# MLP products and transposes as pairs of 128x64 column tiles, and constants from a scan on VectorE

## The chip, the cores and the metric

One core of a Trainium2 chip. The metric is device time of one execution in microseconds (us), a little under 2 us more than the span from first to last instruction that the profile shows. The medians are of all executions; six of these were classed slow (one each in e1, e3, e5 and e10, two in e11), and the ratios leave them out. PE is TensorE's matmuls, PEld its weight loads, DVE is VectorE, ACT is ScalarE, POOL is GpSimd, SP is SyncE.

## The reference

Retention (attention with a decay instead of a softmax) over 8 batches, 8 heads, 576 positions and head size 64, followed by an MLP with the exact GELU over 4,608 tokens, width 512, inner width 2,048.

```python
scores = scale * np.matmul(q, k.transpose(0, 1, 3, 2))
ret = scores * Dmat[None, :, :, :]           # gamma ** (i - j) for i >= j, else 0
attn_out = np.matmul(ret, v)
x = attn_out.transpose(0, 2, 1, 3).reshape(B * S, H * D)
h = x @ w_in
g = 0.5 * h * (1.0 + erf(h / sqrt(2)))
out = g @ w_out
```

## The kernel before

The sequence is cut into 40 chunks of 128 positions (the last of each batch has 64). For each chunk q, k and v are loaded by POOL, q and k are turned (on PE for the first 9 chunks, by DMA transpose after that), and PE computes scores, inner products, running states and a cross term. Their sum, scaled, is xT, the input of the MLP. The MLP products use one level of Strassen-like sums: `hT` is the first product, `fast` the second, `lean` the first one of the last two token blocks. A list schedule written in Python mixes attention groups into the MLP by a modelled clock, so the kernel's instruction order is fixed when it is built.

Three shapes of TensorE array appear. The MLP and the transposes use the whole array:

```python
        tiled(0)                                   # only the schedule's model of a mode change
        hT, tag = bank([128, TOK_BLK], FP32, "hT")
        ...
        for cc in range(N_DM):
            nc.tensor.matmul(hT[:, :hi - lo], lhsT=w[:, cc, o:o + 128], rhs=xT[:, cc, ...],
                             start=(cc == 0), stop=(cc == N_DM - 1))
```

Inner products and states use two column tiles of 128x64, scores and cross four or two tiles of 64x64:

```python
                nc.tensor.matmul(s["o_ps"][64 * e:64 * e + 64, hp, :cs], lhsT=s["vh"][:, 2 * hp + e, :],
                                 rhs=s["ret"][e][:, hp, :cs], ...)          # inner, 128x64
                    nc.tensor.matmul(sc[e][lo:lo + 64, hp, :cs], lhsT=qkT[sl, 1, hp, lo:lo + 64],
                                     rhs=qkT[sl, 0, hp, :cs], ...)          # scores, 64x64
```

The constants (identity, mask, positions, decay factors) are made at the start by POOL, PE and VectorE together; POOL makes the identity between its first two loads:

```python
    nc.gpsimd.dma_start(qk0[:, 1], k[0, :, 0:C, :].rearrange("h s d -> s h d"))
    make_identity(nc, ident)
    nc.gpsimd.dma_start(v0, v[0, :, 0:C, :].rearrange("h s d -> s h d"))
    ...
    nc.gpsimd.iota(pos[:, 0, :], ...)
    nc.gpsimd.affine_select(out=msk[:, 0, :], ...)
```

## Time and profile before

| | before |
|---|---|
| time, median of 3 (range) | 293.27 us (292.81 to 295.05) |
| span of the profiled run | 291.2 us |
| PE busy | 279.8 us, 96% |
| changes of array mode, counted from the matmuls' shapes | 80 |
| first MLP matmul | at 18.0 us |
| instruction fetches of 16 KB | 26 |

The page of the kernel before. Part 1 gives busy time and instruction counts, part 2 tenths of busy time in 40 slices of the span, part 3 a DMA queue with its packets, MB and share of the span.

```profile
span 291.2 us, 8057 instructions
...
PE 279.8 (96%) x3374; PEld 211.3 (73%) x3390; DVE 216.7 (74%) x492; ACT 139.3 (48%) x291; POOL 112.6 (39%) x143
...
PE   6879999999999999999999999999999999999995
...
PEclk9999999999999999999999999999999999999999
...
q8 instruction: 26, 0.43, 0.6%
```

PE is busy everywhere but in the first slices, at full clock.

The timeline of the kernel before around one attention group: start, duration, engine, line, operation, shapes.

```profile
83.83 0.39 PE L389 MATMUL u_ps<-vh,qk_ld 128*64 128x64 bf16 x14
...
84.05 0.62 PE L366 MATMUL o_ps<-ret,vh 128*64 128x128 bf16 x16
...
84.60 0.64 PE L330 MATMUL sc<-qkT 64*64 64x128 bf16 x32
...
85.07 0.39 PE L422 MATMUL o_ps<-qkT,u_sb 64*64 64x128 bf16 x8
...
85.39 0.83 PE L574 MATMUL fast<-w_sum,g 128*128 128x256 bf16 x6
```

The array goes from 128x128 (before the first line) to 128x64, to 64x64 and back: three changes. In single matmuls, the start-to-start time is 109 ns for 256 columns and 202 ns when the next matmul has another shape: 93 ns a change. (The count of 80 takes the one short transpose, 64x128, for a full tile. The trace shows such gaps, 95 ns on entering and 91 ns on leaving it, so 81 is as good a count.)

POOL at the start of the kernel before:

```profile
1.31 1.03 POOL L113 DMA_DIRECT2D qk_ld<-in_k_dram  x1 [0.80 <-POOLq L1008]
2.33 0.23 POOL masks.py:197 MEMSET ident<- 128x128 bf16 x1
2.63 0.29 POOL masks.py:199 TENSOR_SCALAR_AFFINE_SELECT ident<-ident 128x128 bf16<-128x128 bf16 x1
2.87 0.92 POOL L116 DMA_DIRECT2D v_ld<-in_v_dram  x1
...
4.14 0.91 POOL L224 DMA_DIRECT2D qk_ld<-in_q_dram  x1
```

The identity and later the positions and mask hold the loads back by 0.9 us.

### The profile page before, as it was taken

The page shows a single profiled execution, that of the slowest core. Times are in us where ns is not written, and L with a number is a line of the kernel's source. Part 1 is how long each engine was busy: PE and PEld are TensorE (multiplying, and loading weights), DVE is VectorE, ACT ScalarE, POOL GpSimd, SP SyncE. Part 2 cuts the span into 40 slices and gives each one's busy share as a digit, 9 for nine tenths or more (in the row PEclk, how much of TensorE's full clock was granted, in tenths as well). Part 3 has the DMA queues.
Part 4 walks back from the last instruction along what each step waited for, and adds up shares of the span by engine and source line. Part 5 has one row for each costly group of instructions (what it writes and reads, how often), then busy time and mean ns, then how long its engine had stood idle before and what let it go on. Part 6 is the DMA issues. An engine that isn't in the chain of part 4 may idle for free.

```text
span 291.2 us, 8057 instructions
## 1 busy us (share of the span) xinstructions
PE 279.8 (96%) x3374; PEld 211.3 (73%) x3390; DVE 216.7 (74%) x492; ACT 139.3 (48%) x291; POOL 112.6 (39%) x143
## 2 busy tenths in 40 slices
PE   6879999999999999999999999999999999999995
PEld 2555687888988788557865586559854888888884
DVE  5865896928849997997299917979596778995552
ACT  3755584622426721554236523552246438787221
POOL 8978876967366327526743525000000000000000
PEclk9999999999999999999999999999999999999999
DMA  9999999999999999999999999960210000300133
GB/s 87 136 172 185 178 176 186 145 160 138 181 197 188 170 145 149 184 184 159 124 186 175 154 144 157 164 78 2 74 74 0 1 2 0 146 0 3 50 132 108
DMA packets 153605, 35.65 MB, mean 122 GB/s; under 512 B 142305, under 2 KB 149473, under 8 KB 153569
## 3 DMA queue, kind: packets, MB, share of 16 engines
q0 software_dynamic: 117872, 18.23, 91.9%
q1 hardware_dynamic: 35696, 16.91, 33.2%
q8 instruction: 26, 0.43, 0.6%
q14 instruction: 11, 0.08, 0.1%
HBM read 36.70 MB, written 9.44 MB: 158 GB/s over the span
## 4 chain that ended last, share of the span: by engine, by line
PE 81%; DVE 11%; POOL 4%; DMA 2%; issue 1%; POOLq 0%; DVEq 0%
PE fast L574 34%; PE hT L469 29%; PE lean L707 8%; PE sc L330 3%; PE o_ps L366 2%; DVE ret L341 2%; DMA w_in<-in_moe_w_in_dram 2%; PE u_ps L389 2%; PE o_ps L422 2%; POOL qk_ld L224 2%; DVE s L506 2%; DVE s L505 1%; DVE s L508 1%; DVE s L507 1%; DVE xT L434 1%
## 5 line engine op out<-in xcount | busy, mean ns | idle before, releaser
L469 PE MATMUL hT<-xT,w_in 128*128 128x512 bf16 (+5 forms) x646 | 101.1, 309 | 2.5 <-DMA w_in<-in_moe_w_in_dram 1.1
L473 ACT ACTIVATE g<-hT 128x512 bf16<-128x512 f32 (+6 forms) x165 | 73.8, 460 | 51.7 <-PE hT L469 49.9
L469 PEld LDWEIGHTS <-w_in 128*128 128x128 bf16 x660 | 56.0, 98 | 40.8 <-DMA w_in<-in_moe_w_in_dram 2.1
L574 PEld LDWEIGHTS <-s 128*128 128x128 bf16 x576 | 56.0, 98 | 7.4 <-DVE s L506 0.7
L574 PE MATMUL fast<-w_sum,s 128*128 128x256 bf16 x432 | 49.4, 273 | 0.3 <-DVE s L506 0.2
L224 POOL DMA_DIRECT2D qk_ld<-in_q_dram x39 | 33.4, 857 | 33.6 <-DMA qkT<-qk_ld 18.9
L574 PEld LDWEIGHTS <-g 128*128 128x128 bf16 x432 | 41.6, 98 | 5.7
L341 DVE TENSOR_TENSOR ret<-sc,msk 128x512 bf16<-128x512 f32 x64 | 41.0, 683 | 0.9 <-PE sc L330 0.8
L224 POOL DMA_DIRECT2D v_ld<-in_v_dram x39 | 33.2, 853 | 18.4 <-DVE ret L341 4.6
L224 POOL DMA_DIRECT2D qk_ld<-in_k_dram x39 | 33.4, 856 | 10.0 <-DMA v_ld<-in_v_dram 9.0
L574 PE MATMUL fast<-w_out,g 128*128 128x256 bf16 x288 | 33.6, 273 | 0.1
L598 DVE TENSOR_TENSOR o_sb<-fast,u 128x512 f32<-128x512 f32 (+1 forms) x20 | 12.7, 634 | 26.8 <-PE fast L574 16.9
L594 ACT COPY u<-fast 128x512 f32<-128x512 f32 (+1 forms) x20 | 10.9, 544 | 39.6 <-PE fast L574 39.6
L434 DVE TENSOR_TENSOR xT<-o_ps,dq 128x512 bf16<-128x512 f32 (+1 forms) x42 | 24.0, 605 | 0.0
L351 DVE TENSOR_TENSOR vh<-v_ld,dv 128x512 bf16<-128x512 bf16 x32 | 21.3, 682 | 2.7 <-DMA v_ld<-in_v_dram 2.7
L505 DVE TENSOR_TENSOR s<-g 128x512 bf16<-128x512 bf16 x36 | 15.1, 420 | 5.5 <-ACT g L473 5.1
L574 PE MATMUL fast<-w_out,s 128*128 128x256 bf16 x144 | 17.3, 272 | 0.0
L574 PE MATMUL fast<-w_sum,g 128*128 128x256 bf16 x144 | 17.3, 273 | 0.0
L404 ACT CAST u_sb<-run_sum 128x256 bf16<-128x256 f32 x24 | 9.7, 405 | 15.2 <-DVE run_sum L401 11.7
L506 DVE TENSOR_TENSOR s<-s,g 128x512 bf16<-128x512 bf16 x36 | 15.3, 425 | 1.2
L507 DVE TENSOR_TENSOR s<-g 128x512 bf16<-128x512 bf16 x36 | 15.1, 419 | 0.0
L508 DVE TENSOR_TENSOR s<-g,s 128x512 bf16<-128x512 bf16 x36 | 15.1, 418 | 0.0
(85 smaller groups left out, 295.7 us busy)
## 6 DMA issues: line engine op xcount, KB each, us to landing
out_dram<-o_sb SPq DMA_DIRECT2D x16, 512.0 KB, 7.1
qk_ld<-in_k_dram POOLq DMA_DIRECT2D x32, 128.0 KB, 8.9
v_ld<-in_v_dram POOLq DMA_DIRECT2D x32, 128.0 KB, 8.6
qk_ld<-in_q_dram POOLq DMA_DIRECT2D x31, 128.0 KB, 8.9
w_in<-in_moe_w_in_dram POOLq DMA_DIRECT2D x8, 256.0 KB, 7.5
w_out<-in_moe_w_out_dram POOLq DMA_DIRECT2D x8, 256.0 KB, 7.7
out_dram<-o_sb SPq DMA_DIRECT2D x8, 128.0 KB, 1.7
qk_ld<-in_q_dram POOLq DMA_DIRECT2D x8, 64.0 KB, 8.5
```

The source lines that it names most:

```text
L224: nc.gpsimd.dma_start(dst[:cs], src[b, :, c0:c0 + cs, :].rearrange("h s d -> s h d"))
L341: nc.vector.tensor_tensor(r[:cs, :, :cs], sc[e][:cs, :, :cs], msk[:cs, :, :cs].to_broadcast([cs, HP, cs]), op=ALU.mult)
L351: nc.vector.tensor_tensor(vh[:cs], loaded[i][1][:cs], dv[:cs, :, ci:ci + 1].to_broadcast([cs, H, D]), op=ALU.mult)
L434: nc.vector.tensor_tensor(xT[:, :, at:at + hi - lo], s["o_ps"][:, :, lo:hi], dq[:, :, c0 + lo:c0 + hi], op=ALU.mult)
L469: nc.tensor.matmul(hT[:, :hi - lo], lhsT=w[:, cc, o:o + 128], rhs=xT[:, cc, tok0 % RING + lo:tok0 % RING + hi], start=(cc == 0), stop=(cc ...
L473: nc.scalar.activation(g_of(t, m, lo, hi), hT[:, :hi - lo], AF.Gelu)
L505: nc.vector.tensor_tensor(u[:, 0], a[2, 1], a[2, 2], op=ALU.add)
L506: nc.vector.tensor_tensor(u[:, 1], u[:, 0], a[1, 1], op=ALU.subtract)
L507: nc.vector.tensor_tensor(u[:, 2], a[1, 1], a[2, 1], op=ALU.subtract)
L508: nc.vector.tensor_tensor(u[:, 3], a[1, 2], u[:, 1], op=ALU.subtract)
L574: nc.tensor.matmul(acc_[:, p, :], lhsT=left(t, lhs, j, p), rhs=right(rhs, j), start=(fresh and j == 0 and (p == 0 or apart)), stop=(j == N ...
L707: nc.tensor.matmul(acc_[:, p, :], lhsT=left_, rhs=right_, start=(k in (1, 2, 7) and cc == 0 and p == 0), stop=(cc == 1), skip_group_check= ...
```

## The change

Its intent: if MLP and transposes run as pairs of 128x64 tiles, the change between 128x128 and 128x64 falls away and only scores and cross still need one. And if VectorE makes the constants with a scan (a running count along the row), POOL can issue loads at once.

```diff
     def mlp1_step(t, m, lo, hi):
-        tiled(0)
+        tiled(1)
...
-            nc.tensor.matmul(hT[:, :hi - lo], lhsT=w[:, cc, o:o + 128], rhs=xT[...],
-                             start=(cc == 0), stop=(cc == N_DM - 1))
+            for sl in HALVES:                      # slice(0, 64), slice(64, 128)
+                nc.tensor.matmul(hT[sl, :hi - lo], lhsT=w[:, cc, o + sl.start:o + sl.stop], rhs=xT[...],
+                                 start=(cc == 0), stop=(cc == N_DM - 1), skip_group_check=True)
... (the same in the second product, the lean blocks and the transposes)
-    make_identity(nc, ident)
-    nc.gpsimd.dma_start(v0, ...)
+    nc.gpsimd.dma_start(v0, ...)
+    nc.vector.tensor_tensor_scan(row, ones.to_broadcast([128, S]), ones.to_broadcast([128, S]), -1.0,
+                                 op0=ALU.mult, op1=ALU.add)
... (identity, mask and positions from row and its 32x32 transpose; iota, affine_select and
     the product on PE go; six warm-up matmuls at once; three memsets moved behind the first mask)
```

More of the change, by code (lines that the diff above doesn't have):

```diff
@@ L7 @@
 from concourse import bass_utils, mybir
-from concourse.masks import make_identity
 from concourse._compat import with_exitstack
@@ L65 @@
     TR_LEAD = 5
+    POOL_0 = 2.0
+    LAND_0 = (2.9, 4.0, 5.0)
+    CLOCK_0 = 3.2
     PLAN = [(1, 16), (1, 5), (1, 110), (0, 103), (1, 60), (1, 26), (1, 55), (0, 6), (2, 1), (1, 91), (0, 61), (1, 28), (2, 40), (2, 20), (2, 1), (1, 0), (2, 71), (2, 10), (2, 70), (2, 91), (2, 119), (2, 73), (2, 129), (2, 147), (2, 76), (2, 178), (2, 111), (1, 155), (0, 0), (0, 0)]
@@ L113 @@
     nc.gpsimd.dma_start(qk0[:, 1], k[0, :, 0:C, :].rearrange("h s d -> s h d"))
+    nc.gpsimd.dma_start(v0, v[0, :, 0:C, :].rearrange("h s d -> s h d"))
+    ones = const_pool.tile([128, 1], FP32, name="ones")
+    nc.vector.memset(ones, 1.0)
+    row = o_pool.tile([128, S], FP32, tag="o_sb0", name="row", bufs=2)
+    nc.vector.tensor_tensor_scan(row, ones.to_broadcast([128, S]), ones.to_broadcast([128, S]), -1.0,
+                                 op0=ALU.mult, op1=ALU.add)
+    colp = const_pool.tile([128, 1], FP32, name="colp")
+    for n in range(4):
+        nc.vector.memset(colp[32 * n:32 * n + 32], 32.0 * n)
+    turned = const_pool.tile([128, 32], FP32, name="turned")
+    nc.vector.transpose(turned, row[:, :32])
+    nc.vector.tensor_tensor(colp, colp, turned[:, 0:1], op=ALU.add)
     ident = const_pool.tile([128, 128], BF16, name="ident")
-    make_identity(nc, ident)
-    nc.gpsimd.dma_start(v0, v[0, :, 0:C, :].rearrange("h s d -> s h d"))
+    nc.vector.tensor_scalar(ident, row[:, :128], colp, None, op0=ALU.is_equal)
     lg_row = const_pool.tile([128, H, 1], FP32, name="lg_row")
@@ L120 @@
         nc.vector.memset(lg_row[:, h], log_gamma[h])
+    lg_col = const_pool.tile([128, HP], FP32, name="lg_col")
+    for e in range(2):
+        sl = slice(64 * e, 64 * e + 64)
+        nc.vector.tensor_copy(lg_col[sl], lg_row[sl, e::2, 0])
     ln_scale = const_pool.tile([128, 1], FP32, name="ln_scale")
     nc.vector.memset(ln_scale, math.log(scale))
-    msk = const_pool.tile([128, 1, 128], FP32, name="msk")
-    nc.vector.memset(msk, 1.0)
-    pos = const_pool.tile([128, 1, NCH], FP32, name="pos")
-    nc.gpsimd.iota(pos[:, 0, :], pattern=[[C, NCH]], base=0, channel_multiplier=1,
-                   allow_small_or_imprecise_dtypes=True)
-    nc.gpsimd.affine_select(
-        out=msk[:, 0, :], in_=msk[:, 0, :], compare_op=ALU.is_ge, fill=0.0, base=0,
-        pattern=[[1, 128]], channel_multiplier=-1,
-    )
-    lg_col = const_pool.tile([128, HP], FP32, name="lg_col")
-    for h in range(H):
-        e, hp = h % 2, h // 2
-        nc.vector.memset(lg_col[64 * e:64 * e + 64, hp:hp + 1], log_gamma[h])
-    base = const_pool.tile([128, NCH, 1], FP32, name="base")
-    for c in range(NCH):
-        nc.vector.memset(base[:, c], float(C * c))
-    ones = const_pool.tile([128, 128], BF16, name="ones")
-    nc.vector.memset(ones, 1.0)
-    ret_short = [const_pool.tile([128, HP, 128], BF16, name=f"ret_short{e}") for e in range(2)]
-    vh_short = const_pool.tile([128, H, D], BF16, name="vh_short")
-    for t in ret_short + [vh_short]:
-        nc.vector.memset(t, 0.0)
-    diag = const_pool.tile([128, 128], BF16, name="diag")
-    nc.vector.tensor_tensor(diag, ident, pos[:, 0, 0:1].to_broadcast([128, 128]), op=ALU.mult)
+    nc.vector.tensor_copy(qk0[:, 0], first)
+    pos = const_pool.tile([128, 1, NCH], FP32, name="pos")
+    nc.vector.tensor_tensor(pos[:, 0], row[:, 0::C], colp.to_broadcast([128, NCH]), op=ALU.add)
+    arg = const_pool.tile([128, H, NCH], FP32, name="arg")
+    nc.vector.tensor_tensor(arg, lg_row.to_broadcast([128, H, NCH]), pos.to_broadcast([128, H, NCH]), op=ALU.mult)
+    msk = const_pool.tile([128, 1, 128], FP32, name="msk")
+    nc.vector.tensor_scalar(msk[:, 0], row[:, :128], colp, None, op0=ALU.is_ge)
     warm_ps = ps.tile([128, 512], FP32, tag="f", name="warm")
-    row_ps = ps.tile([128, 1, 128], FP32, tag="g", name="row_ps")
     def warm_up(n):
@@ L155, in warm_up @@
             nc.tensor.matmul(warm_ps, lhsT=zeros[:, :128], rhs=zeros, start=True, stop=True)
-    warm_up(4)
-    nc.tensor.matmul(row_ps[:, 0], lhsT=ones, rhs=diag, start=True, stop=True)
-    row = o_pool.tile([128, NCH, 128], FP32, tag="o_sb0", name="row", bufs=2)
-    nc.vector.tensor_tensor(row, row_ps.to_broadcast([128, NCH, 128]), base.to_broadcast([128, NCH, 128]), op=ALU.add)
-    arg = const_pool.tile([128, H, NCH], FP32, name="arg")
-    nc.vector.tensor_tensor(arg, lg_row.to_broadcast([128, H, NCH]), pos.to_broadcast([128, H, NCH]), op=ALU.mult)
+    warm_up(6)
     dv = const_pool.tile([128, H, NCH], FP32, name="dv")
@@ L167 @@
     for hp in range(HP):
-        nc.scalar.activation(dq[:, hp], row.rearrange("p c s -> p (c s)")[:, :S], AF.Exp, scale=lg_col[:, hp:hp + 1])
+        nc.scalar.activation(dq[:, hp], row, AF.Exp, scale=lg_col[:, hp:hp + 1])
     warm_act = const_pool.tile([128, 1], FP32, name="warm_act")
     nc.scalar.activation(warm_act, ln_scale, AF.Gelu)
+    ret_short = [const_pool.tile([128, HP, 128], BF16, name=f"ret_short{e}") for e in range(2)]
+    vh_short = const_pool.tile([128, H, D], BF16, name="vh_short")
     loaded = {}
@@ L178 @@
     dma_at = [0.0]
-    pool_at = [3.3]
+    pool_at = [POOL_0]
     def serve(queues, t, until, landed):
@@ L217, in load_chunk @@
             loaded[i] = (qk0, v0)
-            nc.vector.tensor_copy(qk0[:, 0], first)
-            land_q[i], land_k[i], land_v[i] = on_dve(4.25, 512, 1.5), 5.3, 6.2
+            land_q[i], land_k[i], land_v[i] = on_dve(LAND_0[0], 512, 1.5), LAND_0[1], LAND_0[2]
             return
@@ L276, in bank @@
         return ps.tile(shape, dtype, tag=tag, name=name), tag
-    mode = [0]
+    mode = [1]
+    HALVES = (slice(0, 64), slice(64, 128))
     def tiled(n):
@@ L299, in turn @@
             return
-        tiled(0)
+        tiled(1 if cs == C else 2)
         for j in parts:
@@ L304, in turn @@
             for hp in range(HP):
-                nc.tensor.transpose(ps_[:, hp, :cs], qk[:cs, j, 2 * hp:2 * hp + 2, :], ident[:cs, :cs])
+                for e, sl in enumerate(HALVES):
+                    nc.tensor.transpose(ps_[sl, hp, :cs], qk[:cs, j, 2 * hp + e, :], ident[:cs, :cs])
             clock[0] += 0.23 * cs / C
@@ L464, in mlp1_step @@
         wait(x_ready(tok0 + lo, tok0 + hi))
-        tiled(0)
+        tiled(1)
         hT, tag = bank([128, TOK_BLK], FP32, "hT")
@@ L468, in mlp1_step @@
         for cc in range(N_DM):
-            nc.tensor.matmul(hT[:, :hi - lo], lhsT=w[:, cc, o:o + 128], rhs=xT[:, cc, tok0 % RING + lo:tok0 % RING + hi],
-                             start=(cc == 0), stop=(cc == N_DM - 1))
+            for sl in HALVES:
+                nc.tensor.matmul(hT[sl, :hi - lo], lhsT=w[:, cc, o + sl.start:o + sl.stop],
+                                 rhs=xT[:, cc, tok0 % RING + lo:tok0 % RING + hi],
+                                 start=(cc == 0), stop=(cc == N_DM - 1), skip_group_check=True)
         clock[0] += N_DM * ((hi - lo) / 2400 + 0.0028)
@@ L565, in fast_step @@
         wait(fast_ready(t, n))
-        tiled(0)
+        tiled(1)
         if k in (1, 2, 7) and (p == 0 or apart):
@@ L573, in fast_step @@
         for j in range(N_DF // 2):
-            nc.tensor.matmul(acc_[:, p, :], lhsT=left(t, lhs, j, p), rhs=right(rhs, j),
-                             start=(fresh and j == 0 and (p == 0 or apart)), stop=(j == N_DF // 2 - 1),
-                             skip_group_check=True)
+            for sl in HALVES:
+                nc.tensor.matmul(acc_[sl, p, :], lhsT=left(t, lhs, j, p)[:, sl], rhs=right(rhs, j),
+                                 start=(fresh and j == 0 and (p == 0 or apart)), stop=(j == N_DF // 2 - 1),
+                                 skip_group_check=True)
         clock[0] += 0.1092 * (N_DF // 2)
@@ L691, in lean_step @@
         end = f["end"]
-        tiled(0)
+        tiled(1)
         if k in (1, 2, 7):
@@ L706, in lean_step @@
                 right_ = x_part(t, int(rhs[1]), int(rhs[2]))[:, cc] if rhs[0] == "B" else x_sums[t][int(rhs[1]) - 1][:, cc]
-                nc.tensor.matmul(acc_[:, p, :], lhsT=left_, rhs=right_, start=(k in (1, 2, 7) and cc == 0 and p == 0),
-                                 stop=(cc == 1), skip_group_check=True)
+                for sl in HALVES:
+                    nc.tensor.matmul(acc_[sl, p, :], lhsT=left_[:, sl], rhs=right_,
+                                     start=(k in (1, 2, 7) and cc == 0 and p == 0), stop=(cc == 1), skip_group_check=True)
         clock[0] += 4 * 0.1092
@@ L909, in attend @@
                 masked(new[0])
+            if new[:1] == [0]:
+                for t in ret_short + [vh_short]:
+                    nc.vector.memset(t, 0.0)
+                    on_dve(clock[0], 256, 1.2)
             for j in pend:
@@ L972 @@
     weights_due = [(land_out[7] + 2.0, 0, 4), (land_out[7] + 6.0, 4, 8)]
-    warm_up(2)
-    clock[0] = 4.2
+    clock[0] = CLOCK_0
     while True:
```

## The prediction

> **What bounds the kernel now.** TensorE, except at the start. The page gives PE 96% busy of a 291.2 us span at a granted clock of 1.00, and from 50 us on nearly every slice is 90% or more. The chain of waits that ended last is 81% PE. Reading start-to-start times of single matmuls out of the trace: a full 128x128 matmul costs 216 ns at 512 columns, 109 ns at 256, 56 ns at 128. Summing streaming time over all 3374 recorded matmuls gives about 261 us. About 18 us remains as stalls (some of it records that are missing), 12 us of it before 50 us. There the timeline shows PE waiting for loads; the first w_in tile landed at 17.9 us. The remaining 7.4 us are changes of array mode.
>
> **What a change of mode costs.** [...] 109 ns becomes 202 ns at a change, 216 becomes 309, 82.5 becomes 176. That is 93 ns each. There are 80: about 25 triples (128x128 to 128x64, to 64x64, and back).
>
> **What the change does to PE.** With MLP and most transposes in 128x64, the triple becomes a pair: 27 entries to 64x64 and 27 exits are left, so 24 to 26 changes fall away (one short transpose keeps 64x64). 26 x 93 ns = 2.4 us, all on PE, hence nearly all on the critical path.
>
> **What it adds.** MLP products (about 1,900 matmuls) become pairs, so as many more matmuls and weight loads. [...] I expect no time from it: the inner products in this trace already run as 128x64 pairs, second tile 3 to 4 ns after the first, one pair per 56 ns at 128 columns, as one full matmul takes; the state products manage a pair per 28 ns at 64 columns. At 256 or 512 columns a pair has longer to hide its weight loads. Issue: MLP needs four instructions per 109 ns; attention groups already ran 73 matmuls with their loads in 1.5 us. Instruction fetches (26 packets of 16 KB) become about 40, each taking about 1 us; no stall expected.
>
> **The start.** Before, POOL does the identity between the k and v loads, then iota and mask select; the timeline shows 0.53 us of delay before the v load (2.87 instead of about 2.34) and 0.4 more before the chunk loads (4.14). Both go: later loads are issued about 0.9 us earlier. POOL and DMA feed the chain until w_in lands, so MLP should start about 0.9 us earlier, near 17.1 us. VectorE's own path (diag, row product, row sum, cast of q at 5.56 us) is replaced by a scan of 576 elements[...]; the cast should come near 4 us and first transposes near 4.7 instead of 6.24. That only helps until loads bind.
>
> **Sum.** 293.3 - 2.4 - 0.9 = 290.0 us. Range 288.2 to 291.9. Chances: faster by over 2% 0.05, within 2% 0.92, slower 0.03.
>
> **What would show it.** Changes of mode about 54, each 93 ns; pair periods 109 and 216 ns; first w_in landing near 17.0; PE stalls after 50 us unchanged; span shorter by about 3 us.
>
> **What would make it wrong.** Pairs that cost more than one matmul at 256 or 512 columns (2 ns a pair would be about 4 us); PE starved of instructions; the list schedule, which follows a modelled clock, falling into another order with other waits; the early microsecond lost again to a later load or to VectorE.

The sum is 293.3 (the median of the first three runs) less 2.4 (26 changes of 93 ns) less 0.9 (the start) = 290.0 us. That weight loads can run under matmuls is on the page of the kernel before: PEld is busy 211.3 us beside PE's 279.8 in a span of 291.2.

## The result, and the profile after

| | before | after |
|---|---|---|
| time, median of 4 (the three above and one more; range) | 293.65 us (292.81 to 295.05) | 310.24 us (308.14 to 311.37) |
| span of the profiled run | 291.2 us | 309.3 us |
| mean granted clock | 1.000 | 0.982 |
| changes of mode | 80 | 70 |
| first MLP matmul | 18.0 us | 18.5 us |
| instruction fetches of 16 KB | 26 | 42 |

The ratio is 1.0552 (95% interval 1.0475 to 1.0628). A ratio here is the mean time of one kernel's fast runs over that of the other's of the same rounds, so it is not quite the ratio of the medians.

The same lines of the page, after:

```profile
span 309.3 us, 11987 instructions
...
PE 287.3 (93%) x5353; PEld 238.8 (77%) x5353; DVE 218.5 (71%) x488; ACT 139.5 (45%) x291; POOL 111.9 (36%) x139
...
PE   6999987997779977999999999999999999999995
...
PEclk9999999999989995999999999999999999999999
...
q8 instruction: 42, 0.69, 1.0%
```

PE has holes from the sixth to the sixteenth slice (some 40 to 125 us), the clock dips twice, and afterwards PE is as dense as before. So the pairs as such are not slow. The chain of waits says it best. Before, its last long piece is:

```profile
268.05 20.10 PE fast L574 x184
```

and after:

```profile
285.63 20.10 PE fast L573 x368
```

184 full matmuls and 368 half ones, the same work, take the same 20.10 us: no cost of column tiles shows here.

What are the holes? The timeline of the kernel after, around one of them:

```profile
85.82 1.39 PE L573 MATMUL fast<-w_sum,s 128*64 128x256 bf16 x22
85.93 1.01 PEld L573 LDWEIGHTS <-s 128*64 128x64 bf16 x18
89.38 1.16 PEld L573 LDWEIGHTS <-s 128*64 128x64 bf16 x20 [2.44 <-issue]
89.39 1.40 PE L573 MATMUL fast<-w_sum,s 128*64 128x256 bf16 x18 [2.17 <-issue]
```

"issue" means that PE waited for nothing that the profile shows: no tile, no semaphore. It stops in the middle of one product. Numbering PE's instructions (matmuls, weight loads and the few waits among them) in order of start gives every such hole after 18 us:

```
last start (us)  until the next (us)   number of the next instruction
 44.0            1.05                  1473 = 256 x 5 + 193
 50.6            1.20                  1729 = 256 x 6 + 193
 59.0            0.40                  1985 = 256 x 7 + 193
 66.2            0.73                  2241 = 256 x 8 + 193
 71.9            2.10                  2497 = 256 x 9 + 193
 79.7            1.83                  2753 = 256 x 10 + 193
 86.9            2.44                  3009 = 256 x 11 + 193
 95.6            0.50                  3265 = 256 x 12 + 193
101.4            0.68                  3521 = 256 x 13 + 193
108.2            1.10                  3777 = 256 x 14 + 193
114.8            3.46                  4033 = 256 x 15 + 193
sum             15.49
```

The holes are exactly 256 instructions apart, or one page, as I call it, eleven times. The page of the profile lists an instruction queue, q8, with packets of 16 KB: 42 of them for the 10,714 PE instructions in the trace of the kernel after, or 255 instructions a packet, and 26 for 6,772 in the kernel before, or 260. So a packet is read here as the fetch of one page. A page of 256 instructions is 128 full matmuls with their weight loads; at 256 columns it lasts 128 x 109 ns = 14 us. As pairs it lasts 64 x 109 ns = 7 us, and less where attention runs (73 matmuls with their loads in 1.5 us).

The trace of DMA packets ties the holes to the fetch directly. Each of the eleven holes ends 1.3 to 1.6 us after a packet of 16 KB on the instruction queue has ended; each of the six in e3 (below, with full tiles) ends 1.2 to 1.6 us after one.

The difference of the two profiled spans, 18.1 us, can be added up from the traces: the holes, 15.5 us less some 0.1 us of ordinary spacing each, make 14.4; around and after the two longest, the clock record has half speed from 90.2 to 93.6 and from 117.5 to 124.3 us, of which PE worked 9.4 us, so lost 4.7; the first MLP matmul came 0.5 later; the changes of mode after it are 48 instead of 69, worth -21 x 93 ns = -2.0. Together 17.6 us.

The half clock followed idle time of PE. From last start to next start PE stood 2.4 us at 86.9 us, and the record is at 0.5 from 90.2 to 93.6 us; it stood 3.5 us at 114.8 us, and the record is at 0.5 from 117.5 to 124.3 us. In both stretches a pair of 256 columns takes 213 ns and not 109. In e1 (below) 2.4 us without PE work was followed by 3.4 us of half clock as well, but 2.1 us at 71.9 us in this run, 3.0 us in e2 and 3.5 us in e5 (at 91.8 us) were not. So the length of one hole did not decide. Windows of the kernel after: engine busy time and, third from the end, the granted clock.

```profile
core 0: us, PE busy (x) PEld busy (x) DVE busy (x) ACT busy (x) POOL busy (x), PEclk, DMA share, GB/s
60.00:80.00 20.00, 17.63 (x378) 16.61 (x372) 11.97 (x28) 4.42 (x11) 11.20 (x13) 1.00 2.07 159
80.00:100.00 20.00, 16.00 (x338) 14.94 (x340) 7.55 (x14) 5.71 (x19) 9.15 (x11) 0.91 1.84 143
100.00:126.00 26.00, 21.47 (x433) 17.99 (x430) 16.94 (x38) 9.50 (x26) 8.41 (x12) 0.87 1.82 144
126.00:200.00 74.00, 74.00 (x1384) 58.10 (x1382) 55.58 (x114) 30.43 (x55) 34.09 (x41) 1.00 1.76 149
```

and of the kernel before:

```profile
60.00:80.00 20.00, 19.89 (x259) 17.79 (x254) 13.99 (x31) 6.30 (x19) 10.96 (x13) 1.00 1.92 158
80.00:100.00 20.00, 20.00 (x323) 16.08 (x321) 15.36 (x29) 10.07 (x25) 12.11 (x15) 1.00 1.77 189
100.00:126.00 26.00, 25.73 (x370) 19.18 (x370) 22.65 (x49) 10.14 (x24) 12.57 (x15) 1.00 1.83 161
126.00:200.00 74.00, 73.63 (x905) 50.05 (x911) 56.06 (x125) 32.49 (x58) 27.20 (x33) 1.00 1.70 145
```

The loss lies between 40 and 126 us; at 126 to 200 us the kernel after keeps PE full, with 1,384 matmuls in place of 905.

The loads were issued early as predicted. POOL after:

```profile
1.24 1.02 POOL L115 DMA_DIRECT2D qk_ld<-in_k_dram  x1 [0.80 <-POOLq L1011]
2.25 0.90 POOL L116 DMA_DIRECT2D v_ld<-in_v_dram  x1
3.12 0.90 POOL L218 DMA_DIRECT2D qk_ld<-in_q_dram  x1
```

The first w_in tile landed at 16.9 us instead of 17.9. The first MLP matmul came half a microsecond later all the same.

### The profile page after: what moved, and what is told of

The parts are those of the page before. It is cut to its first block, busy times and chain, and to the rows that moved or that the text cites. A ratio compares the mean times of both kernels' runs of the same rounds, so it can differ in the third digit from the quotient of the medians.

```text
span 309.3 us, 11987 instructions
## 1 busy us (share of the span) xinstructions
PE 287.3 (93%) x5353; PEld 238.8 (77%) x5353; DVE 218.5 (71%) x488; ACT 139.5 (45%) x291; POOL 111.9 (36%) x139
## 4 chain that ended last, share of the span: by engine, by line
PE 87%; DVE 7%; issue 5%; DVEq 0%
PE fast L573 37%; PE hT L466 30%; PE lean L707 7%; PE sc L326 4%; PE o_ps L362 3%; PE o_ps L418 2%; PE qk_ps L301 1%; PE warm L890 1%; PE u_ps L385 1%; DVE ret L337 1%; DVE u L722 1%; DVE s L504 1%; DVE xT L430 1%; DVE s L506 0%; DVE s L503 0%
## 5 line engine op out<-in xcount | busy, mean ns | idle before, releaser
L466 PE MATMUL hT<-xT,w_in 128*64 128x512 bf16 (+6 forms) x1320 | 102.7, 311 | 4.4 <-issue 3.3
L466 PEld LDWEIGHTS <-w_in 128*64 128x64 bf16 x1320 | 64.1, 110 | 36.3 <-issue 4.7
L573 PEld LDWEIGHTS <-s 128*64 128x64 bf16 x1152 | 64.5, 113 | 4.3 <-issue 3.2
L573 PE MATMUL fast<-w_sum,s 128*64 128x256 bf16 x864 | 51.3, 277 | 2.6 <-issue 2.6
L573 PEld LDWEIGHTS <-g 128*64 128x64 bf16 x864 | 47.8, 113 | 7.7 <-issue 6.0
L573 PE MATMUL fast<-w_out,g 128*64 128x256 bf16 x576 | 36.4, 284 | 3.3 <-issue 3.2
L593 ACT COPY u<-fast 128x512 f32<-128x512 f32 (+1 forms) x20 | 10.9, 543 | 42.5 <-PE fast L573 42.5
L573 PE MATMUL fast<-w_sum,g 128*64 128x256 bf16 x288 | 17.6, 274 | 1.8 <-issue 1.8
L573 PE MATMUL fast<-w_out,s 128*64 128x256 bf16 x288 | 18.6, 283 | 0.0
L326 PE MATMUL sc<-qkT 64*64 64x128 bf16 (+1 forms) x576 | 13.8, 220 | 1.4 <-issue 1.3
```

Source lines behind the costliest of these rows:

```text
L466: nc.tensor.matmul(hT[sl, :hi - lo], lhsT=w[:, cc, o + sl.start:o + sl.stop], rhs=xT[:, cc, tok0 % RING + lo:tok0 % RING + hi], start=(cc ...
L573: nc.tensor.matmul(acc_[sl, p, :], lhsT=left(t, lhs, j, p)[:, sl], rhs=right(rhs, j), start=(fresh and j == 0 and (p == 0 or apart)), stop ...
```

## The experiments

The theory: PE is starved of instructions, because pairs double their number and the fetch of the next page waits behind the other DMA traffic. The rivals: column tiles stall PE by themselves, or the new start does the harm. Each result is correct unless noted. "Before" in a row is the median of the kernel before on the same chip. A hole is counted after 18 us where PE stood over 0.25 us longer than the last matmul streams and nothing is named as its releaser; the offset in the page differs by a few instructions from kernel to kernel (189 to 193) and is fixed within one.

| run | median us | before | ratio (95% interval) | holes at steps of 256 PE instructions: number, sum us (profiled run) |
|---|---|---|---|---|
| e1_start_only | 296.51 | 293.64 | 1.0085 (1.0038 to 1.0131) | 0 |
| e2_pairs_only | 308.33 | 293.64 | 1.0485 (1.0423 to 1.0546) | 10, 14.7 |
| e3_full_split | 307.24 | 293.64 | 1.0436 (1.0380 to 1.0493) | 6, 10.2 |
| e4_half_loads (wrong result) | 295.05 | 293.64 | 1.0033 (0.9978 to 1.0089) | 3, 3.5 |
| e5_late_traffic | 310.20 | 293.56 | 1.0552 (1.0475 to 1.0628) | 9, 15.7 |
| e6_mlp1_pairs | 301.48 | 293.56 | 1.0268 (1.0214 to 1.0321) | 5, 6.5 |
| e7_warm_pairs | 310.07 | 293.56 | 1.0532 (1.0477 to 1.0587) | 8, 14.3 |
| e9_late_pairs | 295.75 | 293.56 | 1.0046 (1.0002 to 1.0089) | 2, 2.0 |
| e10_cap4 | 301.30 | 293.65 | 1.0220 (1.0161 to 1.0278) | 3, 3.4 |
| e11_warm_cap4 | 303.61 | 293.65 | 1.0265 (1.0207 to 1.0323) | 2, 3.0 |
| e12_before_cap4 | 302.38 | 293.65 | 1.0273 (1.0232 to 1.0314) | 0 |
| e13_warm_cap3 | 322.21 | 293.65 | 1.0950 (1.0890 to 1.1011) | 1, 1.3 |
| e14_before_half (wrong) | 293.31 | 293.30 | 1.0007 (0.9984 to 1.0031) | 0 |
| e15_start_half (wrong) | 292.83 | 293.30 | 0.9982 (0.9957 to 1.0007) | 0 |
| e16_warm_half (wrong) | 293.55 | 293.30 | 1.0013 (0.9989 to 1.0038) | 3, 3.0 |
| e17_warm_cap6 | 309.71 | 293.30 | 1.0540 (1.0497 to 1.0583) | 9, 15.0 |

### The two parts alone

e1_start_only, the kernel after with full tiles:

```diff
-            for sl in HALVES: ... hT[sl, ...] lhsT=w[:, cc, o + sl.start:o + sl.stop] ...
+            nc.tensor.matmul(hT[:, :hi - lo], lhsT=w[:, cc, o:o + 128], ...)   # and so everywhere
```

> The changed kernel with full 128x128 matmuls for MLP and transposes again; the new constants stay. Theory (the loss is TensorE starved of instructions, because the pairs double its instruction count): no idle of PE at every 256th instruction, clock 1.0 after the warm-up, time 292 to 295 us, as before the change. Second reading (the new start itself does harm, through the clock or another order): over 300 us. If my early microsecond had been real it would be near 292.5; if the cold clock at the start eats it, 293 to 294.5.

No holes; 296.51 us (0.85% over the kernel before by the fast runs), above what I had expected. The first MLP matmul comes at 17.1 us, 0.9 us earlier, and that lead holds until about 120 us. Then, in the profiled run, VectorE waits 3.9 us for a v load that POOL issued about 2 us later than in the kernel before, PE waits for VectorE, and the clock falls to half for 3.4 us. Another run, with a mean clock of 1.000, still took 295.42 us, so the half clock is only part of the excess. The waits of the profiled run between 118 and 134 us (total, times, longest):

```profile
DVE vh L346 <- DMA v_ld<-in_v_dram: 3.9, 1, 3.9
...
PE hT L464 <- DVE u_sb L402: 2.0, 1, 2.0
```

e2_pairs_only, the kernel before with `for sl in HALVES` in the four places and its old constants:

> The kernel before with the pairs alone; its old constants stay. Theory (starved of instructions): 306 to 313 us, PE idle for 0.4 to 3.5 us at steps of exactly 256 PE instructions between about 40 and 125 us, and half clock after the longest of them. If start and pairs did harm only together: under 300 us.

308.33 us, ten holes, all at 256k + 193. The pairs carry the loss; the new start is not needed for it. In this profiled run (305.72 us) the clock stayed at full speed, so the holes suffice for most of the loss. The half clock that I had expected after the longest of them did not come in this run; the mean clocks of the other three were 0.983 to 0.989.

### Number of instructions or shape of the tiles?

e3_full_split keeps 128x128 and cuts the moving operand in two, so the counts nearly match those of the pairs:

```diff
-                nc.tensor.matmul(acc_[:, p, :], lhsT=left(t, lhs, j, p), rhs=right(rhs, j), ...)
+            for a_ in (0, COL // 2):
+                nc.tensor.matmul(acc_[:, p, a_:a_ + COL // 2], lhsT=left(t, lhs, j, p),
+                                 rhs=right(rhs, j)[:, a_:a_ + COL // 2], ...)
```

> The kernel before, every MLP matmul still full 128x128 but cut into two by columns of the moving operand, so PE has as many instructions as in the changed kernel (10,566 rows against 10,708) and no column tiles. Streaming alone grows by about 3 ns for each of some 1,300 cut 256-column matmuls and 1 to 2 ns for the rest, 4 to 5 us: 298 us. Theory (number of instructions): the same idle at every 256th PE instruction, 306 to 322 us. Rival (128x64 tiling itself stalls PE[...]): no such idle, 296 to 300 us.

307.24 us and six holes, again at 256k + 193, 0.8 to 2.8 us long. (The streaming time in the expectation is an estimate that follows from start-to-start times in the kernel before: 3 ns is 2 x 56 - 109 for 256 columns, and 512 columns give 2 x 109 - 216 = 2 ns.) PE in this run, with full tiles (`128*128`):

```profile
81.39 0.89 PE L578 MATMUL fast<-w_sum,s 128*128 128x128 bf16 x13
84.75 1.46 PE L578 MATMUL fast<-w_sum,s 128*128 128x128 bf16 x23 [2.47 <-issue]
```

The number of instructions makes the holes; column tiles are not needed for them. This run parts the theory from its rival.

### Does the fetch wait behind other traffic?

e4_half_loads is the kernel after with half of the rows of q, k and v set to zero by POOL, not loaded, from the tenth chunk on:

```diff
-            nc.gpsimd.dma_start(dst[:cs], src[b, :, c0:c0 + cs, :]...)
+            rows = cs if i < N_LD else cs // 2
+            if rows < cs:
+                nc.gpsimd.memset(dst[rows:cs], 0.0)
+            nc.gpsimd.dma_start(dst[:rows], src[b, :, c0:c0 + rows, :]...)
```

> The changed kernel, wrong on purpose: from the tenth chunk on, half the rows of q, k and v are not loaded but set to zero by POOL, which halves that queue's traffic after about 45 us; the instructions of PE are the same. Theory (the fetch of the next 256 instructions waits in crowded DMA engines): idle at the 256-instruction steps falls from about 15 us to under 6, no half clock, 291 to 300 us. Rival (128x64 tiling itself, whatever the DMA does): 306 to 312 us as the changed kernel.

295.05 us: same PE instructions, less traffic, and the holes shrink from 15.5 to 3.5 us. On average 3.0 loads of POOL were in flight between 60 and 120 us, where the kernel after has 6.1.

e5_late_traffic adds 48 loads at the end, where the kernel after has no holes:

> The changed kernel with 48 more loads of a v chunk into a constant that is no longer needed, issued by POOL after its last load, so from about 200 us on, where the changed kernel has quiet DMA and no idle of PE at the 256-instruction steps. Theory (fetch of instructions behind other DMA traffic): such idle now appears after 200 us as well, if the loads keep several in flight, 3 or more of them and 2 to 10 us longer than the changed kernel (312 to 320 us). If the early idle comes from something of the early phase other than traffic (small matmuls, weights): none after 200 us, 308 to 312 us. If the extra loads run one at a time, little traffic and no answer.

No hole appeared after 125 us. By what I had written down this is the outcome against the theory (308 to 312 us), since three or more loads were kept in flight: the 48 loads go to four slots of one constant, each waiting for an earlier one to land, and some 3.6 were in flight on average, where the crowded phase has mostly 4 to 8. That 3.6 are too few to delay a fetch by a whole page is a reading made after the run; it is no test at full crowd. It still shows a measure: from a fetch's estimated request to the start of its packet. (The request is not in the trace. I estimate it as the moment when PE starts the 28th instruction before a page's end, or, where PE stood at the page's end, as the moment when it goes on. The 28 is a choice within what the quiet stretch shows: after 205 us, with the loads over, the kernel after's 14 packets start between 37 instructions before a page's end and 7 after it.) In the kernel after this wait is 3.1 to 5.4 us between 60 and 120 us, and at most 1.0 us after 205 us; with these late loads in flight 0.3 to 2.8 us. The same estimate for the kernel before, with page ends at the same offset, gives 3.6 to 5.3 us between 60 and 120 us: the fetch was about as late there, but a page lasted longer, 8.9 us on average from 60 to 126 us (952 matmuls and 945 weight loads in 66 us), and PE showed no hole.

A less indirect figure for the whole round trip: when PE ran dry at two page ends in a row, I take the time from going on after the first to going on after the second for one fetch. In the table of holes: 74.0 to 81.5, to 89.4, to 96.1, to 102.1, to 109.3, to 118.3 us, so 5.9 to 8.9 us, against 7 us that a page of 256-column pairs lasts. It is the sum of three parts: 3.1 to 5.4 us of waiting, 0.9 to 2.1 us for the packet itself, and the 1.3 to 1.6 us from its end until PE goes on.

e6_mlp1_pairs puts only the first product and the transposes in pairs, and the second back to full tiles:

> The changed kernel with pairs only in the first MLP product and the transposes; the second product and the lean blocks go back to full 128x128. 77 changes of mode instead of 56. Theory (rate of instructions against the time of a fetch): 512-column pairs use 256 instructions in 13.8 us, as slow as full matmuls at 256 columns, so the idle in the stretches of the second product (59 to 115 us) goes and at most the ones near 44 and 50 us stay, where narrow first products run: 0 to 4 us of idle, 294 to 300 us. Rival (any 128x64 MLP pair stalls): about half of the loss stays, 301 to 305 us.

301.48 us, above what I had expected, with five holes. I had thought of the first product as 512 columns wide (64 pairs of 216 ns, 13.8 us a page). Until about 105 us it also runs narrower: one hole, at 90.9 us, follows 48 half matmuls of it in 2.6 us (27 ns for each instruction, loads counted, as in the second product) and an attention group. By the number this is the outcome that I had written down for the rival (301 to 305 us, about half of the loss stays), not the theory's (294 to 300 us). The trace speaks for the theory all the same: the holes lie at steps of 256 instructions and are ended by no releaser. But that the narrow first products use up a page fast enough is a reading that came after the run.

### The start

e7_warm_pairs is the kernel after with its warm-up matmuls in pairs as well:

> The changed kernel with its warm-up matmuls as 128x64 pairs too. In the trace of the changed kernel 15 of 17 changes between 128x128 and 128x64 lie in the first 20 us, around warm-up matmuls that kept 128x128. Theory (these changes, at half clock, ate the early microsecond): first MLP matmul near 17.1 us instead of 18.5, 1 to 1.5 us shorter than the changed kernel, 307 to 310 us. If it is the clock's own luck: first MLP matmul stays at 18 us or later.

The first MLP matmul came at 17.5 us instead of 18.5, and the 70 changes of mode became 56. So much of the lost start came from 14 changes between warm-up matmuls (128x128) and transposes (128x64). (The clock record of the kernel after begins at 11.7 us. The half clock that the expectation names is read from the warm-up matmuls before 4 us: they start 427 ns apart, where 512 columns take 216 ns later.) The total stayed at 310.07 us: I had expected a shorter one, and the gain is not seen behind the holes.

### Holding the loads back

In the three cap runs, POOL copies one element of the load four (six, three) before, so that it waits until that has landed:

```diff
+        if len(issued) >= 40:                       # from the tenth chunk on
+            nc.gpsimd.tensor_copy(touch, issued[-4])
+        issued.append(dst)
         nc.gpsimd.dma_start(dst[:cs], ...)
```

> The changed kernel, correct, but from the tenth chunk on POOL issues a load only when the load four before it has landed (it copies one element of it first), so at most 4 are in flight instead of about 7.5. In the traces so far a fetch of instructions waits 3 to 5.5 us with 7 to 8 loads in flight, 1 to 2.8 us with 3.6, under 1 us with none. Theory (the fetch waits its turn behind loads in flight): waits fall to 2 to 3 us, idle at the 256-instruction steps after 60 us falls from some 13 us to under 4, 293 to 299 us. Rival (the fetch is slow whatever the number in flight, by the rate of DMA alone): 306 to 312 us. If the cap starves the kernel of chunks: waits for loads instead, over 300 us with no idle at the steps.

> The same cap with the warm-up matmuls as pairs (first MLP matmul near 17.4 us). A candidate for the best version. Theory: 1 us less than the run with the cap alone, 292 to 298 us; below 292 only if the idle near 44 and 50 us, where the cap doesn't reach, goes too.

> Control: the kernel before with the cap. It has no idle for instructions, so the cap should change nothing but load timing: 292.5 to 295.5 us. If it is over 297 us, the cap itself costs time and the two runs above are to be read against this one.

> At most 3 loads in flight, warm-ups as pairs. Theory: fetch waits 1 to 2.5 us and no idle at the steps after 60 us; but 3 loads in about 4 us is nearer to what the kernel consumes (93 loads in about 145 us), so waits for chunks may come instead: 291 to 300 us.

The cap of 4 (301.30 us, above the 293 to 299 us that I had expected) does to the fetch what the theory says: the median wait between 60 and 120 us falls from 4.7 to 2.5 us, the holes from 15.5 to 3.4 us. But the chunks now come late: the control, full tiles with the same cap, is 2.7% slower than without it. I had expected nothing there. Its windows show where:

```profile
60.00:90.00 30.00, 29.15 (x405) 25.79 (x404) 19.58 (x42) 9.33 (x27) 19.26 (x38) 1.00 2.01 173
90.00:118.00 28.00, 22.21 (x314) 16.91 (x313) 20.18 (x44) 9.99 (x28) 18.02 (x34) 0.88 2.09 143
118.00:200.00 82.00, 81.89 (x1019) 55.34 (x1018) 60.74 (x126) 34.63 (x62) 48.74 (x92) 1.00 1.84 148
```

Between 88 and 120 us PE waits 5.8 us for VectorE, VectorE 6.3 us for v loads, and POOL's copies 10.9 us for loads to land. Read against this control, the pairs under the cap (301.30 us) are no slower than full tiles (302.38 us; the intervals overlap): both kernels suffer from the late chunks, and a loss of the pairs' own no longer shows. The version with pairs for warm-ups, 303.61 us, was not better, and a cap of 3 starves the kernel (322.21 us, where I had expected at most 300; the "about 4 us" for three loads was my estimate, and the nearest measured figure is e5's late loads, 4.4 us from issue to landing in the median with 3.6 in flight).

### Controls for the half loads, and a milder cap

> The kernel before with half of the rows of q, k and v not loaded from the tenth chunk on (wrong on purpose). The control for the changed kernel with half loads, 295.05 us. It has no idle for instructions to lose, so only the 1 to 2 us of waits for loads between 50 and 195 us can go: 291.5 to 294 us.

> The new start with full tiles and half loads (wrong on purpose). If the start's early 0.9 us is lost to late loads, it is kept here: 0.5 to 1.2 us less than the kernel before with half loads. If the start harms by itself: 1 us or more above it.

> Pairs, new start, warm-ups as pairs, half loads (wrong on purpose). The theory's whole sum without the crowd of loads: 2.2 us less for 24 changes of mode, 0.5 us for the start, plus 0 to 4 us of idle for instructions that half loads leave (3.5 us in the earlier run): 290 to 295 us, and, idle at the 256-instruction steps taken off, 2 to 3 us below the kernel before with half loads. If pairs cost something of their own: not below it with that idle taken off.

With half loads, the kernel before takes 293.31 us, pairs with the new start and pair warm-ups 293.55 us. The profiled run of the latter has three holes of 3.0 us together, 2.7 us beyond ordinary spacing. Without them it would be near 290.9 us, 2.4 us below its control, where 2.7 us had been expected (2.2 for the changes of mode, 0.5 for the start). It is an estimate from one profiled run, and no run shows that time, but it suggests that pairs and start are worth about what I had predicted once instructions arrive in time. The start alone with half loads is 0.5 us below its control: in the direction of "the early microsecond is lost to late loads", but the two intervals overlap, so this is not clear of noise.

> Pairs everywhere, new start, at most 6 loads in flight from the tenth chunk on; correct. A candidate for the best version. Fetch waits of 2.5 to 4 us, 4 to 9 us of idle for instructions, little waiting for chunks: 297 to 304 us. It beats the kernel before only if both waits nearly vanish, which I don't expect.

309.71 us with 15.0 us of holes: worse than I had expected. With six loads allowed, the estimated wait of a fetch between 60 and 120 us is 4.7 us, as without a cap. The cap of 6 lowered the loads in flight in that stretch only from 6.1 on average to 5.2, the cap of 4 to 3.5.

### A version that beats both?

e9_late_pairs is the kernel before, with pairs only from token block 3 on, where the kernel after had no holes, and in the lean blocks:

```diff
-        tiled(0)
+        tiled(1 if t >= 3 else 0)
...
+            for sl in HALVES if t >= 3 else WHOLE:
```

> The kernel before with its old start and pairs only for token blocks 3 to 8 and the lean blocks, where the changed kernel showed no idle at the 256-instruction steps. 70 changes of mode instead of 80. Theory: no such idle or nearly none, 10 x 93 ns = 0.9 us less than before: 292.3 to 293.3 us. If pairs cost something by themselves: 294.5 us or more.

295.75 us, 0.46% above the kernel before. Ten changes of mode are gone (0.9 us), but the profiled run has two holes of 1.0 us each, at 98 and 153 us, and a stretch of half clock at 18 to 22 us. I had written 294.5 us or more down as the sign that pairs cost something by themselves. Taking the holes (1.8 us beyond ordinary spacing) and the half clock (1.5 us) off the profiled run's 296.32 us leaves an estimated 293.0 us, as the theory had it, but two runs with a mean clock of 1.000 took 295.62 and 295.94 us and were not profiled, so this run alone does not rule a small cost out. No correct version that I ran beats the kernel before.

## Why the prediction was wrong

- **The step that failed** is this one: "Instruction fetches (26 packets of 16 KB) become about 40, each taking about 1 us; no stall expected." The count was right (42). The time was mis-sized: 1 us is how long the packet itself takes once it moves (0.9 to 2.1 us in the trace of the kernel after). It first waits an estimated 3 to 5.4 us where loads are crowded, PE goes on only 1.3 to 1.6 us after it has ended, and the round trip, from one refill to the next, was 5.9 to 8.9 us. I compared 1 us with the 7 us of a page; the right comparison was 6 to 9 us with 7 us or less. It cost 14.4 us of idle and, after it, 4.7 us lost to half clock. e3 (nearly the same count, full tiles) shows that the count is the cause; e4 and e10 (fewer loads in flight, holes of 3.5 and 3.4 us in place of 15.5) show that traffic is what makes the fetch late.
- **The evidence on issue that I cited proved too little.** That attention groups ran 73 matmuls in 1.5 us showed a burst of some 146 instructions, fewer than the 256 of one page. It said nothing of a rate kept up over several pages.
- **Mode changes**: right in kind and size (93 ns each), but the kernel after has 70, not 54. Warm-ups stayed 128x128, and 14 changes around them came in; with pairs there too it is 56.
- **"a pair costs what one matmul costs"**: right; 20.10 us on both sides for the last piece.
- **The early microsecond**: the loads came as early as predicted, and in e1 the first product began 0.9 us earlier. In the kernel after it was lost before the first product to changes of mode around warm-ups; in e1 it was lost later, at about 130 us, to a late v load and half clock. Half loads kept 0.5 us of it, within noise. VectorE's own path was quicker by less than predicted: the scan took 1.36 us, the cast came at 5.02 us and not near 4, and the first transposes at 5.51 us and not near 4.7.
- The warning "PE starved of instructions" stood under what would make the prediction wrong. It was named and not costed.

What stays open: which traffic holds the fetch most (chunk loads, DMA transposes and stores share the crowded time, and no run took the transposes away), how many instructions PE has at hand at once (no run measured it), and why a cap of 6 helps nothing while a cap of 4 does (5.2 against 3.5 loads in flight is a hint, not a test).

## What to carry to other kernels

Before doubling PE's instruction count as here, compare: 256 instructions times the time that each will last (here 7 us as pairs, 14 us as full matmuls) against the round trip of a fetch under the kernel's own DMA load (here 5.9 to 8.9 us), not against the duration of its packet (0.9 to 2.1 us). A hole ended by "issue" with no releaser, coming back every 256 instructions, was that fetch in these runs. Where a change must add instructions, look for stretches in which the fetch waits little: in the kernel after it waited an estimated 3.1 to 5.4 us between 60 and 120 us, where most of the holes lay, and at most 1.0 us after 205 us, where there were none.
